# First loads on two queues, scores and values of half 1 in other banks, and head steps laid out unit by unit: a linear-attention and two-MLP kernel on one core

## The chip, the cores and the metric

The kernel runs on one core of a Trainium2 chip. The metric is device microseconds (us) of one execution, as a median of several; lower is better. The core has five engines that each run their own queue in order and wait for one another through semaphores: TensorE (PE; its weight loads are PEld), VectorE (DVE), ScalarE (ACT), GpSimd (POOL) and SyncE (SP), which issues most transfers. "Granted clock" is the share of TensorE's full speed that the chip allowed in a stretch; its two levels are 1.2 and 2.4 GHz, 0.5 and 1.0 in the rows.

## What is computed

Three stages follow one another. Inputs are q, k, v, alpha of 4 x 8 x 768 x 48 (batch, head, step, dimension); there are 3072 tokens of width 384.

```python
for t in range(S):                                   # gated linear attention
    state = alpha[:, :, t, :, None] * state + einsum(k[:, :, t], v[:, :, t])
    y[:, :, t] = einsum(q[:, :, t], state)
h = x @ w_in                                         # 384 -> 2048
P = a[0] + a[1]*h + a[2]*h**2 + a[3]*h**3
Q = 1.0 + abs(b[0])*abs(h) + abs(b[1])*h**2
x2 = (P / (Q + 1e-06)) @ w_out                       # 2048 -> 384
h = x2 @ w_in2                                       # 384 -> 1024
so = h * softmax(h); ln = normalise(so) * g_ln
out = ln @ w_out2                                    # 1024 -> 384
```

The weights arrive as 64-bit floats and are turned into a pair of 32-bit numbers, high and low, by integer steps on the chip; a product of two such pairs takes three matmuls.

## The kernel before

**Attention.** The 768 steps are cut into six chunks of 128 (c), and each chunk into two halves by batch, so half i has chunk i // 2; halves 2c and 2c + 1 must be done before chunk c goes on. A half's raw alpha, k and q come in by `a_load` (twelve transfers of 96 KB, all on SP), its v by `v_load`. Halves 0 and 1 are turned by TensorE (`a_turn`, products with a unit matrix), and DVE runs two scans per step over them. Halves 2 to 11 are turned by DVE itself (`a_prep`, which is `a_dve`: stream transposes, two long scans), then written to HBM and read back in another layout (`a_move_qk`, `a_move`). `a_pe` then makes the scores `sc`, copies them to `A` (ACT) and masks them (POOL), makes the values `y` and splits them into the chunk's activation `xt`, high part by ACT and low part by DVE, and updates the state `Sbd`. Eight PSUM banks are shared: three for `x2p`, three (`ps_hp`, tag "h") for the up-matmuls' `hp`, two (`ps_ap`, tag "at") for attention.

**First MLP.** 96 units follow, u = 16 c + f: unit u takes 128 of the 2048 columns for the 512 tokens of chunk c. `m_up` is nine matmuls into one bank, a rational function on ACT, DVE and POOL (three DVE steps in even units up to 22, lines 599, 604, 605; four in the others, lines 607, 610, 611, 612), and the pair `gh`, `gl`. `m_down` of the same unit is nine matmuls, laid four units later.

**Weights of the first MLP.** They come in four groups, one for each four units of a chunk (`w1_group`, seven tiles each: three of `w_in`, four of `w_out`). A tile is loaded as 64-bit numbers into a staging buffer, joined by three DVE instructions (`split_w`, lines 526, 529, 530), rounded by ACT and subtracted by POOL. There are two staging buffers `st`; while `stage["wide"]` is set, every second tile goes into a third one, `lent`, borrowed from a later group's place. In the kernel before, group 0, group 1 and the preparation of half 2 lie ahead of unit 0, and groups 2 and 3 lie in units 0 to 7.

**Order.** A planner sorts each engine's queue when the kernel is built, from the order of the code; `tc.issue_after` ties an instruction behind another. `half_steps(i)` lays one step of `a_pe(i)` and two of the next half's preparation into each unit from unit 2 of a half chunk on. After the units comes the second MLP, and out goes each tile of 128 tokens in four transfers (`n_out`).

## Time and profile before

| what | us |
|---|---|
| median of 3 runs | 805.89 (803.84 to 811.34) |
| profiled execution | 805.28 |
| its span | 803.5 |
| PE busy | 736.9 (92%) |
| DVE busy | 641.5 (80%) |
| ACT busy | 535.4 (67%) |
| POOL busy | 365.4 (45%) |

The profile is of one execution. Its own time is 1.8 us longer than its span, which is what lies around it. Busy shares are means over stages with different limits, so they have to be read stage by stage.

### The profile page before, as it was taken

Reading aid. Unit: us, or ns where it says so; the run is one execution under the profiler, and the core shown is the slowest. Engines: PE = TensorE matmul, PEld = TensorE weight load, DVE = VectorE, ACT = ScalarE, POOL = GpSimd, SP = SyncE. Lnnn points to the kernel's source line nnn. Section 1 sums busy time; section 2 is a strip of 40 time slices with the busy share of each in tenths; the row PEclk is TensorE's granted clock in tenths of the full one; section 3 lists DMA queues with packets and bytes.
Section 4 is the critical chain, followed back from the end, with each engine's and each line's share of the span. In section 5 each row is a group of like instructions: output and inputs, shape, how many; then the busy total and the mean of one; then the engine's idle time right before and its main releaser. Section 6 shows DMA issues by size and latency. Waiting matters only on the chain. (4 is left out here: it accounts for less than half of the span.)

```text
span 803.5 us, 13909 instructions
## 1 busy us (share of the span) xinstructions
PE 736.9 (92%) x4976; PEld 613.0 (76%) x4976; DVE 641.5 (80%) x1110; ACT 535.4 (67%) x983; POOL 365.4 (45%) x306
## 2 busy tenths in 40 slices
PE   4777786889999989999999999999999999999995
PEld 4665565667787767877777778888888989998995
DVE  6994999998889988979898976657877698777730
ACT  2324756678786868778887879788775555554631
POOL 3254757777654545445354334243233524352321
PEclk9757797999999998999999999999999999999998
DMA  7878229362764467363927151360013544541552
GB/s 171 174 176 241 86 84 231 100 163 76 225 162 147 89 199 174 116 151 110 226 80 179 45 124 29 117 278 0 1 40 100 143 105 110 134 113 48 130 128 61
DMA packets 87279, 101.75 MB, mean 127 GB/s; under 512 B 34464, under 2 KB 63136, under 8 KB 87200
## 3 DMA queue, kind: packets, MB, share of 16 engines
q1 hardware_dynamic: 87200, 100.77, 47.7%
q8 instruction: 41, 0.67, 0.4%
q14 instruction: 38, 0.31, 0.1%
HBM read 60.59 MB, written 27.56 MB: 110 GB/s over the span
## 5 line engine op out<-in xcount | busy, mean ns | idle before, releaser
L581 PE MATMUL hp<-xt,g 128*128 128x512 f32 x864 | 229.7, 408 | 24.9 <-DVE p L612 20.8
L581 PEld LDWEIGHTS hp<-xt,g 128*128 128x128 f32 x864 | 165.3, 195 | 68.0 <-DVE p L612 26.9
L615 POOL TENSOR_TENSOR gl<-p,gh 128x512 fp32r<-128x512 f32 x96 | 131.1, 1366 | 175.3 <-ACT gh L614 109.8
L627 PE MATMUL x2p<-gh,g 128*128 128x512 f32 x576 | 196.3, 397 | 0.0
L627 PEld LDWEIGHTS x2p<-gh,g 128*128 128x128 f32 x576 | 109.2, 190 | 25.4 <-issue 0.6
L627 PE MATMUL x2p<-gl,g 128*128 128x512 f32 x288 | 113.2, 393 | 0.4 <-POOL gl L615 0.4
L765 PE MATMUL op<-w2oh,room 128*128 128x384 f32 x384 | 101.6, 339 | 0.2 <-DVEq L1012 0.2
L757 POOL TENSOR_TENSOR room<-room,room 128x1024 fp32r<-128x1024 f32 x22 | 54.2, 2469 | 102.8 <-ACT room L756 87.8
L610 DVE SCALAR_TENSOR_TENSOR w<-w,co,hp 128x512 f32<-128x512 f32 x84 | 61.7, 735 | 42.7 <-ACT hp L609 42.4
L701 PE MATMUL h<-w2ih,x 128*128 128x512 f32 x288 | 90.8, 394 | 0.0
L588 ACT ACTIVATE p<-hp,co 128x512 f32<-128x512 f32 x96 | 66.0, 687 | 13.6 <-POOL gl L615 13.1
L607 DVE SCALAR_TENSOR_TENSOR p<-p,co,hp 128x512 f32<-128x512 f32 x84 | 61.6, 734 | 16.2 <-ACT p L588 15.8
L609 ACT ACTIVATE hp<-ah 128x512 f32<-128x512 f32 x84 | 50.2, 598 | 33.9 <-DVE p L607 33.3
L589 ACT ACTIVATE w<-ah,co 128x512 f32<-128x512 f32 x96 | 69.3, 722 | 4.4 <-DVE hp L611 4.2
L614 ACT ACTIVATE gh<-p 128x512 fp32r<-128x512 f32 x96 | 59.9, 624 | 18.3 <-DVE p L612 8.0
L765 PEld LDWEIGHTS op<-w2oh,room 128*128 128x128 f32 x384 | 70.1, 188 | 1.4 <-DVEq L1012 0.5
L586 ACT ACTIVATE ah<-hp 128x512 f32<-128x512 f32 x96 | 56.6, 590 | 13.7 <-PE hp L581 13.5
L765 PE MATMUL op<-w2ol,room 128*128 128x384 f32 x192 | 65.0, 338 | 0.0
L627 PEld LDWEIGHTS x2p<-gl,g 128*128 128x128 f32 x288 | 54.3, 189 | 12.6 <-POOL gl L615 0.8
L612 DVE SCALAR_TENSOR_TENSOR p<-p,co,hp 128x512 f32<-128x512 f32 x84 | 62.1, 740 | 1.0
L701 PEld LDWEIGHTS h<-w2ih,x 128*128 128x128 f32 x288 | 53.8, 188 | 11.8
L608 ACT ACTIVATE ah<-w,co 128x512 f32<-128x512 f32 x84 | 60.5, 720 | 1.3
(165 smaller groups left out, 1286.4 us busy)
## 6 DMA issues: line engine op xcount, KB each, us to landing
room<-room SPq DMA_DIRECT2D x96, 128.0 KB, 2.3
qk_d<-qk SPq DMA_DIRECT2D x10, 771.0 KB, 4.7
st<-in_moe_w_in_dram SPq DMA_DIRECT2D x15, 512.0 KB, 5.1
st<-in_moe_w_out_dram SPq DMA_DIRECT2D x20, 384.0 KB, 3.8
qks<-qk_d SPq DMA_DIRECT2D x20, 257.0 KB, 5.3
x<-x_d SPq DMA_DIRECT2D x18, 256.0 KB, 3.3
out_dram<-o SPq DMA_DIRECT2D x96, 48.0 KB, 1.6
ra<-in_alpha_dram SPq DMA_DIRECT2D x44, 96.0 KB, 3.3
```

What stands on the lines that cost most here:

```text
L581: last["PE", u] = nc.tensor.matmul(hp, lhsT=w[:, kt, 128 * o:128 * o + 128], rhs=xts[c][:, kt, xx, :], start=(kt == 0 and w is hi and xx = ...
L588: nc.scalar.activation(p, hp, AF.Square, bias=co[:, 7:8])
L589: nc.scalar.activation(w, ah, AF.Square, bias=co[:, 6:7])
L607: nc.vector.scalar_tensor_tensor(p, p, a1, hp, ALU.add, ALU.mult)
L608: nc.scalar.activation(ah, w, AF.Ln, bias=rest)
L610: nc.vector.scalar_tensor_tensor(w, w, rest, hp, ALU.add, ALU.mult)
L612: fin[u] = nc.vector.scalar_tensor_tensor(p, p, a0, hp, ALU.add, ALU.mult)
L614: last["ACT", u] = nc.scalar.activation(gh, p, AF.Copy)
L615: last["POOL", u] = nc.gpsimd.tensor_tensor(gl, p, gh[:].bitcast(F32), ALU.subtract)
L627: nc.tensor.matmul(x2ps[c][d], lhsT=w[:, o, 128 * d:128 * d + 128], rhs=gg, start=(f == 0 and w is hi and gg is gh), stop=(f == NF1 - 1 an ...
L701: nc.tensor.matmul(hp[:, 512 * n:512 * n + 512], lhsT=x2s[c][:, kt, x, CH * b:CH * b + CH], rhs=w2[w][:, kt, 512 * n:512 * n + 512], start ...
L765: nc.tensor.matmul(op, lhsT=x[:, 128 * f:128 * f + 128], rhs=w2[w][:, f, :], start=(f == 0 and x is hi and w == "oh"), stop=(f == NF2 - 1 ...
```

## The change

First, the raw loads of halves 0 and 1 go ahead of all weights, half of them on ACT's queue (`a_load` has a queue argument), and two of the four transfers of the very last output tile go out by ACT's queue. Second, nineteen instructions of `consts()`, which make coefficients from the six numbers of a and b, move from DVE to POOL, where one of them becomes two; one reciprocal stays on DVE. Third, half 1's scores and values take the three "h" banks. Fourth, weight groups 1, 2 and 3 lie in units 0 to 3, 4 to 7 and 8 to 11, each two tiles a unit, tied behind the last step of the unit before (`G1 = 1`); only groups 0 and 1 use the third staging buffer. Fifth, `script()` lays preparation (p), score and value steps (s) and moves (q, m, l) of halves 2 to 5 into named units up to 25; from unit 26 on the old rule goes on.

```diff
--- before.py
+++ after.py
@@ -70,17 +70,17 @@
     BETA = 2.0
     FASTS = (0, 20)
     GE = 80
-    NA = 5
     PRE = (1, 1, 0, 0)
     GP = 2
     GS = 2
-    G1 = 99
+    G1 = 1
     G2 = 3
     MIX = lambda u: u < 24 and u % 2 == 0
     EARLY = (9, 11, 13, 15)
     SKIP = (5, 7, 11)
     AHEAD = 3
     LATE = 2
+    FREE = 26
     U2, TP = 16, 0.3
     assert (B, H, D, CH) == (4, 8, 48, 128)
 
@@ -117,26 +117,28 @@
         nc.scalar.activation(cf[:, 0:1], bb[:, 1:2], AF.Abs)
         nc.scalar.activation(cf[:, 1:2], ab[:, 3:4], AF.Abs)
         nc.scalar.activation(lin[:, 0:1], bb[:, 0:1], AF.Abs)
-        nc.vector.tensor_scalar(sign, ab[:, 3:4], 0.0, 2.0, ALU.is_ge, ALU.mult)
...
-        nc.vector.tensor_scalar(cf, cf, C_MIN, None, ALU.max)
+        g = nc.gpsimd
+        g.tensor_scalar(sign, ab[:, 3:4], 0.0, 2.0, ALU.is_ge, ALU.mult)
...
+        g.tensor_scalar(cf, cf, C_MIN, None, ALU.max)
         nc.vector.reciprocal(rc, cf)
-        nc.vector.scalar_tensor_tensor(beta, lin, 0.5, rc, ALU.mult, ALU.mult)
-        nc.vector.tensor_tensor(t, beta, beta, ALU.mult)
...
+        g.tensor_tensor(beta, lin, rc, ALU.mult)
+        g.tensor_scalar(beta, beta, 0.5, None, ALU.mult)
+        g.tensor_tensor(t, beta, beta, ALU.mult)
...
@@ -249,7 +251,7 @@
             c, bp = divmod(i, 2)
             return c, 2 * bp + x // 2, 4 * (x % 2)
 
-        def a_load(i, names=("ra", "rk", "rq")):
+        def a_load(i, names=("ra", "rk", "rq"), queue=nc.sync):
             for x, (src, nm) in enumerate(((alpha, "ra"), (k, "rk"), (q, "rq"))):
                 if nm not in names:
                     continue
@@ -263,7 +265,7 @@
                     nc.gpsimd.memset(t[:, 16 * D:], 1.0)
                 for y in range(B):
                     c, b, h = slot(i, y)
-                    nc.sync.dma_start(
+                    queue.dma_start(
                         out=t[32 * y:32 * y + 32, :16 * D].rearrange("p (h x) -> p h x", h=4),
                         in_=src[b, h:h + 4, CH * c:CH * c + CH, :].rearrange("h (j r) d -> j h (r d)", r=4),
                     )
@@ -412,9 +414,10 @@
             c, bp = divmod(i, 2)
             vt = vts.pop(i)
             hf = half(i)
+            own = (ps_hp, "h") if i == 1 else (ps_ap, "at")
             A = {}
             for p in range(2):
-                sc = [ps_ap.tile([128, B, CH], F32, name="sc", tag="at") for j in range(2)]
+                sc = [own[0].tile([128, B, CH], F32, name="sc", tag=own[1]) for j in range(2)]
                 for x in range(B):
                     for j in range(2):
                         nc.tensor.matmul(
@@ -425,7 +428,7 @@
                 for j in range(2):
                     t = A[p, j] = ap_.tile([128, B, CH], F32, name="A", tag=f"A{p}{j}")
                     nc.scalar.activation(t, sc[j], AF.Copy)
-                    nc.gpsimd.affine_select(
+                    marks[i, "A"] = nc.gpsimd.affine_select(
                         out=t, in_=t, pattern=[[0, B], [1, CH]], compare_op=ALU.is_ge, fill=0.0, base=0,
                         channel_multiplier=-1,
                     )
@@ -434,7 +437,7 @@
             nc.gpsimd.tensor_copy(end, hf.ends[:, :, :, 0])
             ends = _view(end[:], 0, [[2, B], [1, 2], [0, D]])
 
-            y2 = [ps_ap.tile([128, n, 2 * CH], F32, name="y", tag="at") for n in (2, 1)]
+            y2 = [own[0].tile([128, n, 2 * CH], F32, name="y", tag=own[1]) for n in (2, 1)]
             begun = set()
 
             def put(m, x, w, r, last):
@@ -688,6 +691,7 @@
                 area[n] = moe_pool.tile([128, GW], F32R if n == 3 else F32, name=f"room{n}", tag=f"g{n}")
             return area[n][:, o:o + size]
 
+        NS = NCH * B
         lnT = {}
         st2 = {}
 
@@ -774,7 +778,7 @@
             nc.scalar.activation(o, op, AF.Copy)
             to = out.rearrange("(b c q j) d -> c q b j d", b=B, c=NCH, q=4)[c, qq]
             for b in range(B):
-                nc.sync.dma_start(out=to[b], in_=o[32 * b:32 * b + 32])
+                (nc.scalar if s == NS - 1 and b % 2 else nc.sync).dma_start(out=to[b], in_=o[32 * b:32 * b + 32])
 
         def n_tile(s):
             n_up(s)
@@ -794,28 +798,27 @@
 
         if fast:
             stage["wide"] = True
+            _run(a_load(0, ("ra",)), a_load(0, ("rk",), nc.scalar), a_load(1, ("ra",), nc.scalar))
+            _run(a_load(0, ("rq",)), a_load(1, ("rk",)), a_load(1, ("rq",), nc.scalar))
+            v_load(0)
+            nc.gpsimd.memset(Sbd, 0.0)
+            _run(a_turn(0))
+            pe0, pe1 = a_pe(0), a_pe(1)
+            take(pe0, 2)
+            _run(a_turn(1))
+            take(pe0, 1)
+            consts()
+            v_load(1)
+            take(pe1, 3)
             pre = w1_group(0)
-            _run(a_load(0))
-            take(pre, PRE[0])
-            v_load(0)
-            consts()
-            take(pre, PRE[1])
-            _run(a_load(1))
-            take(pre, PRE[2])
-            v_load(1)
-            take(pre, PRE[3])
-            nc.gpsimd.memset(Sbd, 0.0)
-            _run(a_turn(0), a_pe(0), a_turn(1), a_pe(1), pre)
-            clear()
-            pre = w1_group(1)
-            take(pre, NA)
+            with tc.issue_after(marks[1, 0, 0].ins):
+                take(pre, KT)
+                with tc.issue_after(marks[1, "A"].ins):
+                    _run(pre)
+            _run(pe0, pe1)
+            with tc.issue_after(marks[1, "A"].ins):
+                clear()
             _run(a_load(2, ("ra", "rk")))
-            with tc.issue_after(marks[0, 1].ins):
-                _run(a_prep(2))
-            _run(a_move_qk(2))
-            _run(a_enter(2), pre)
-            _run(a_load(3, ("ra", "rk")))
-            stage["wide"] = False
         else:
             for n in range(NG):
                 _run(w1_group(n))
@@ -854,15 +857,38 @@
                     return
                 yield
 
+        def script():
+
+            plan = {
+                2: "p2 p2", 3: "p2 p2", 4: "p2 p2 q2 m2 l3", 5: "p3 p3", 6: "p3 p3", 7: "p3 p3 s2", 8: "s2",
+                9: "s2 q3 l4", 10: "s2 m3", 12: "s3", 13: "s3", 14: "s3", 15: "s3", 16: "p4 p4", 17: "p4 p4",
+                18: "p4 p4 q4 m4 l5", 20: "p5 p5", 21: "s4 p5 p5", 22: "s4 p5 p5", 23: "s4 q5 l6", 24: "s4 m5",
+            }
+            ps = {i: a_prep(i) for i in (2, 3, 4, 5)}
+            ss = {i: a_pe(i) for i in (2, 3, 4)}
+            for u in range(FREE):
+                for w in plan.get(u, "").split():
+                    kind, i = w[0], int(w[1])
+                    with pin(GS if kind == "p" else GP):
+                        if kind in "ps":
+                            next((ps if kind == "p" else ss)[i], None)
+                        else:
+                            _run({
+                                "q": a_move_qk, "m": a_move, "l": lambda i: a_load(i, ("ra", "rk")),
+                            }[kind](i))
+                yield
+            for g in (*ps.values(), *ss.values()):
+                _run(g)
+
         split2 = w2_split() if fast else iter(())
         tp = 0.0
-        side = iter(())
+        side = script() if fast else iter(())
         tail = None
         prep = iter(())
         for u in range(NU + LAG):
             c, f = divmod(u, NF1)
             now[0] = u
-            if f % (NF1 // 2) == LATE and u < NU:
+            if f % (NF1 // 2) == LATE and FREE <= u < NU:
                 _run(side)
                 i = 2 * c + 2 + f // (NF1 // 2)
                 side = half_steps(i) if fast and i < NH else iter(())
@@ -877,7 +903,8 @@
                 if fast and u < NF1:
                     if f % 4 == 0:
                         _run(prep)
-                        prep = w1_group(f // 4 + 2) if f < 8 else iter(())
+                        stage["wide"] = f == 0
+                        prep = w1_group(f // 4 + 1) if f < 12 else iter(())
                     with later(G1):
                         take(prep, 1)
                 m_up(u)
@@ -907,7 +934,6 @@
         ph2["ps_o"] = end.enter_context(tc.tile_pool(name="ps_o", bufs=2, space=PSUM, side="left", reuse_waits="tile"))
         ph2["ha"] = end.enter_context(tc.tile_pool(name="ps_ha", bufs=1, space=PSUM, side="left", reuse_waits="tile"))
         ph2["hb"] = end.enter_context(tc.tile_pool(name="ps_hb", bufs=1, space=PSUM, side="left", reuse_waits="tile"))
-        NS = NCH * B
         done = 0
         cut = 0
         for s in range(len(EARLY), NS):
```

In the lists below, names are the program's with buffer numbers; line numbers of the changed kernel are 2 or 3 higher (526, 529, 530 become 529, 532, 533; 599 becomes 602; 128 becomes 129).

DVE in the second step of half 0. `co`, `ab`, `bad` are the coefficients, `ft` and `st` or `lent` a weight tile, `tp`, `Pp`, `Rp` the scans. Before:

```order
L530 SCALAR_TENSOR_TENSOR ft<-st,ft 128x512
L375 TENSOR_SCALAR qks<-Pp 128x4
L121 TENSOR_SCALAR co<-co 128x1
L126 TENSOR_SCALAR bad<-co 128x2
L383 TENSOR_TENSOR qks<-tp,Pp 128x4x128
L376 RECIPROCAL Rp<-qks 128x4
L122 TENSOR_TENSOR co<-ab,co 128x1
L123 TENSOR_TENSOR co<-ab,co 128x1
L124 TENSOR_TENSOR co<-ab,co 128x1
L127 TENSOR_SCALAR co<-co 128x2
L526 TENSOR_SCALAR ft<-lent_173 128x512
L378 SCALAR_TENSOR_TENSOR Rp<-tp,Rp,zero 128x127 x4
```

Now:

```order
L377 TENSOR_SCALAR qks<-Pp 128x4
L378 RECIPROCAL Rp<-qks 128x4
L380 SCALAR_TENSOR_TENSOR Rp<-tp,Rp,zero 128x127 x4
L129 RECIPROCAL co<-co 128x2
L384 TENSOR_TENSOR qks<-tp,Rp 128x4x128
L385 TENSOR_TENSOR qks<-tp,Pp 128x4x128
L376 SCALAR_TENSOR_TENSOR Pp<-tp,zero 128x128 x4
```

The coefficients and the first two weight tiles are gone from between half 0's steps; the reciprocal of `co` stands ahead of the two products that give half 0's k and q.

DVE where group 0 ends and group 1 begins, with the staging buffer `lent`. Before:

```order
L526 TENSOR_SCALAR ft_624<-lent2_173 128x512
L320 TENSOR_TENSOR qk_685<-qk_685,alT_111 128x2x3x128
L529 SCALAR_TENSOR_TENSOR ft_624<-lent2_173,ft_624 128x512
L290 STREAM_TRANSPOSE qk_685<-rq_678 128x2x4x32
L526 TENSOR_SCALAR ft_631<-st_632 128x512
L324 STREAM_TRANSPOSE alT_111<-qk_685 128x3x4x32 x2
L295 STREAM_TRANSPOSE qk_685<-rq_678 128x4x32 x2
L530 SCALAR_TENSOR_TENSOR ft_624<-lent2_173,ft_624 128x512
L529 SCALAR_TENSOR_TENSOR ft_631<-st_632,ft_631 128x512
L290 STREAM_TRANSPOSE qk_685<-rq_678 128x2x4x32
L530 SCALAR_TENSOR_TENSOR ft_631<-st_632,ft_631 128x512
L526 TENSOR_SCALAR ft_639<-lent2_173 128x512
```

Now (`u`, `Sbd` the state of half 0, `xt`, `y` the output of half 1):

```order
L532 SCALAR_TENSOR_TENSOR ft_535<-st_536,ft_535 128x384
L497 TENSOR_TENSOR Sbd_114<-u_570,end_361 48x8x48 x2
L533 SCALAR_TENSOR_TENSOR ft_535<-st_536,ft_535 128x384
L529 TENSOR_SCALAR ft_543<-lent2_273 128x384
L532 SCALAR_TENSOR_TENSOR ft_543<-lent2_273,ft_543 128x384
L533 SCALAR_TENSOR_TENSOR ft_543<-lent2_273,ft_543 128x384
L474 TENSOR_TENSOR xt_397<-y_466,xt_397 128x2x256
L529 TENSOR_SCALAR ft_550<-st_551 128x384
L474 TENSOR_TENSOR xt_397<-y_467,xt_397 128x256
L532 SCALAR_TENSOR_TENSOR ft_550<-st_551,ft_550 128x384
L533 SCALAR_TENSOR_TENSOR ft_550<-st_551,ft_550 128x384
L529 TENSOR_SCALAR ft_635<-lent2_273 128x512
```

Half 2's transposes and scans (`qk`, `alT`) are gone from between the tiles; two uses of `lent` are now two tiles apart with only half 1's output between them.

DVE in groups 2 and 3, where `hp`, `p`, `w` are a unit's function. Before, in units 5 to 8:

```order
L526 TENSOR_SCALAR ft_960<-st_961 128x512
L607 SCALAR_TENSOR_TENSOR p_1252<-p_1252,co_85,hp_1240 128x512
L612 SCALAR_TENSOR_TENSOR p_1111<-p_1111,co_85,hp_1099 128x512
L529 SCALAR_TENSOR_TENSOR ft_960<-st_961,ft_960 128x512
L605 SCALAR_TENSOR_TENSOR p_1192<-w_1191,hp_1180 128x512
L610 SCALAR_TENSOR_TENSOR w_1251<-w_1251,co_85,hp_1240 128x512
L530 SCALAR_TENSOR_TENSOR ft_960<-st_961,ft_960 128x512
L526 TENSOR_SCALAR ft_995<-st_996 128x512
L611 SCALAR_TENSOR_TENSOR hp_1240<-w_1251,hp_1240 128x512
L529 SCALAR_TENSOR_TENSOR ft_995<-st_996,ft_995 128x512
L612 SCALAR_TENSOR_TENSOR p_1252<-p_1252,co_85,hp_1240 128x512
L599 SCALAR_TENSOR_TENSOR hp_1275<-p_1287,co_85,hp_1275 128x512
```

Now, around unit 8's and 9's first steps:

```order
L532 SCALAR_TENSOR_TENSOR ft_1002<-st_1003,ft_1002 128x384
L533 SCALAR_TENSOR_TENSOR ft_1002<-st_1003,ft_1002 128x384
L602 SCALAR_TENSOR_TENSOR hp_1109<-p_1121,co_85,hp_1109 128x512
L610 SCALAR_TENSOR_TENSOR p_1189<-p_1189,co_85,hp_1177 128x512
L529 TENSOR_SCALAR ft_1030<-st_1031 128x384
L532 SCALAR_TENSOR_TENSOR ft_1030<-st_1031,ft_1030 128x384
L533 SCALAR_TENSOR_TENSOR ft_1030<-st_1031,ft_1030 128x384
L529 TENSOR_SCALAR ft_1101<-st_1102 128x512
L532 SCALAR_TENSOR_TENSOR ft_1101<-st_1102,ft_1101 128x512
L533 SCALAR_TENSOR_TENSOR ft_1101<-st_1102,ft_1101 128x512
L607 SCALAR_TENSOR_TENSOR hp_1109<-hp_1109,co_85,ah_1119 128x512
L613 SCALAR_TENSOR_TENSOR w_1188<-w_1188,co_85,hp_1177 128x512
```

Tiles that stood one by one between steps of units stand in rows of two and more, all through the two `st` buffers.

## Rows read from the trace of the kernel before

**Rows 1.** Busy time by stretch, all engines, granted clock and DMA share

```profile
core 0: us, PE busy (x) PEld busy (x) DVE busy (x) ACT busy (x) POOL busy (x), PEclk, DMA share, GB/s
0.00:6.50 6.50, 1.95 (x16) 1.60 (x16) 0.77 (x8) 2.31 (x3) 3.83 (x18) 1.00 0.56 145
6.50:37.20 30.70, 20.01 (x273) 17.10 (x272) 28.01 (x79) 7.46 (x20) 6.99 (x9) 0.85 0.89 189
37.20:61.60 24.40, 17.95 (x144) 15.47 (x144) 22.81 (x40) 7.84 (x18) 13.62 (x10) 0.56 0.68 166
61.60:86.80 25.20, 16.55 (x91) 13.13 (x91) 16.01 (x28) 11.09 (x21) 10.59 (x10) 0.71 0.73 200
86.80:187.60 100.80, 85.92 (x626) 67.33 (x626) 94.88 (x145) 69.70 (x128) 71.36 (x61) 0.92 0.51 131
187.60:261.70 74.10, 71.12 (x579) 57.40 (x578) 68.62 (x110) 58.64 (x108) 43.89 (x39) 0.98 0.55 160
```

**Rows 2.** Waits of DVE, 0 to 240 us: total, times, longest

```profile
DVE p L607 <- ACT p L588: 6.2, 5, 1.9
```

**Rows 3.** DVE in order of time, 58 to 92 us: start, duration, what

```profile
62.72 0.82 DVE L526 TENSOR_SCALAR ft<-lent 128x512 int32<-128x512 int32 x1 [2.28 <-DMA lent<-in_moe_w_in_dram]
63.57 0.69 DVE L529 SCALAR_TENSOR_TENSOR ft<-lent,ft 128x512 int32<-128x512 int32 x1
...
70.29 0.36 DVE L526 TENSOR_SCALAR ft<-lent 128x384 int32<-128x384 int32 x1 [1.89 <-DMA lent<-in_moe_w_out_dram]
...
78.73 1.13 DVE L526 TENSOR_SCALAR ft<-lent 128x384 int32<-128x384 int32 x1 [5.93 <-DMA lent<-in_moe_w_out_dram]
...
86.17 0.68 DVE L605 SCALAR_TENSOR_TENSOR p<-w,hp 128x512 f32<-128x512 f32 x1
```

**Rows 4.** DVE in order of time, 14 to 28 us, lines of consts()

```profile
16.15 0.17 DVE L126 TENSOR_SCALAR bad<-co 128x2 f32<-128x2 f32 x1 [1.22 <-ACT co L117]
...
16.91 1.18 DVE L122 TENSOR_TENSOR co<-ab,co 128x1 f32<-128x1 f32 x1
18.02 0.14 DVE L123 TENSOR_TENSOR co<-ab,co 128x1 f32<-128x1 f32 x1
18.09 0.59 DVE L124 TENSOR_TENSOR co<-ab,co 128x1 f32<-128x1 f32 x1
...
20.96 0.13 DVE L128 RECIPROCAL co<-co 128x2 f32<-128x2 f32 x1
...
25.73 0.73 DVE L134 TENSOR_TENSOR co<-co 128x2 f32<-128x2 f32 x1
...
27.15 0.48 DVE L136 TENSOR_TENSOR co<-co 128x2 f32<-128x2 f32 x1
```

**Rows 5.** PE in order of time, 40 to 120 us

```profile
48.17 4.86 PE L420 MATMUL sc<-lent 48*128 48x128 f32 x24 [2.06 <-DVE Sbd L494]
...
61.64 1.35 PE L581 MATMUL hp<-xt,g 128*128 128x512 f32 x3 [2.75 <-ACT xt L470]
...
92.32 1.34 PE L420 MATMUL sc<-qks 48*128 48x128 f32 x8
...
100.57 0.87 PE L444 MATMUL y<-qks,Sbd 128*32 128x128 f32 x24
...
103.77 2.36 PE L581 MATMUL hp<-xt,g 128*128 128x512 f32 x9
...
115.53 1.14 PE L481 MATMUL u<-vns,kns 128*64 128x48 f32 x32
```

**Rows 6.** DMA issues: queue, count, KB each, median us to landing

```profile
st<-in_moe_w_in_dram SPq DMA_DIRECT2D x15, 512.0 KB, 5.1
st<-in_moe_w_out_dram SPq DMA_DIRECT2D x20, 384.0 KB, 3.8
...
lent<-in_moe_w_out_dram SPq DMA_DIRECT2D x4, 384.0 KB, 5.7
```

**Rows 7.** SP's last transfers in order of time, 790 us to the end

```profile
791.10 6.82 SPq L777 DMA_DIRECT2D out_dram<-o  x8
```

More of the change, by code (lines that the diff above doesn't have):

```diff
@@ L135, in consts @@
[L135 to L139 removed]
+        g = nc.gpsimd
+        g.tensor_scalar(sign, ab[:, 3:4], 0.0, 2.0, ALU.is_ge, ALU.mult)
+        g.tensor_scalar(sign, sign, 1.0, None, ALU.subtract)
+        g.tensor_tensor(lin[:, 1:2], ab[:, 2:3], sign, ALU.mult)
@@ L141 @@
+        g.tensor_scalar(bad[:, 4 * NCH + 2:], t, BETA * BETA, None, ALU.is_gt)
+        g.tensor_scalar(beta, beta, B_MAX, -B_MAX, ALU.min, ALU.max)
+        g.tensor_tensor(t, beta, beta, ALU.mult)
+        g.tensor_tensor(base, base, rc, ALU.mult)
+        g.tensor_tensor(rest, base, t, ALU.subtract)
+        g.tensor_tensor(a0s, a0s, rc[:, 1:2], ALU.mult)
+        g.tensor_tensor(back, cf[:, 1:2], rc[:, 0:1], ALU.mult)
+        g.tensor_tensor(back, back, sign, ALU.mult)
     flag = const.tile([1, 1], I32, name="flag")
```

20 lines of the change are left out of this document (5 added, 15 removed).

## The prediction

> **What bounds the kernel now.** I read the stretches of busy time first and follow DVE and PE from row to row [rows 1]. From 187.6 us on both are full: PE 71.1 of 74.1 us, DVE 68.6. Ahead of that PE is not full: it is busy 85.9 of the 100.8 us from 86.8 to 187.6 and 54.5 of the 80.3 us from 6.5 to 86.8, and much of that at the lower clock (0.56 in 37.2 to 61.6, that is, mostly the 1.2 GHz level). DVE is the engine that is full: 28.0 of 30.7, 22.8 of 24.4, 94.9 of 100.8 us. It has one hole, the stretch from 61.6 to 86.8, where it works 16.0 of 25.2 us. So up to 187.6 us the time is DVE's work plus DVE's waits, and what the change saves ahead of that point is passed on to the end by engines that are full from there, in an order of work that the change leaves alone from unit 26 on.
>
> The waits of DVE come next. In the hole stand three waits of 2.28, 1.89 and 5.93 us, all for a transfer into `lent` [rows 3]; they make 10.1 of the 9.2 + 1.6 us that DVE idles from 37.2 to 86.8. After that only short waits of units for ACT are left (6.2 us in five, [rows 2]). Where the chain of PE looks bad it is not the bound: half 1's scores wait 2.06 us for a bank and run at 0.2 us each, and the first up-matmul starts at 61.64 after a wait for `xt` [rows 5], while DVE is busy 22.8 of 24.4 us in just that stretch. Starting unit 0 earlier is therefore worth nothing by itself; it lets DVE do units' steps and leave tiles and preparation for later, and the sum of its work stays.
>
> **The change part by part**, against the profiled execution's 805.3 us.
>
> *Removed: waits for `lent` in the hole, -10.1 us.* They came while half 2's results went to HBM and back and tiles were loaded with little else for DVE to do. Half 2's preparation now stands behind unit 2, so the round trip is not beside these loads. What replaces them is costed below.
>
> *Removed: coefficients on DVE, -4.0 us.* Four long ones take 1.18 + 0.59 + 0.73 + 0.48 = 3.0 us; fifteen short ones last 0.14 us but the next starts 0.07 us later (18.02 to 18.09), 1.05 us [rows 4]. The wait of 1.22 us for ACT ahead of line 126 goes too: -1.2. The other end: on POOL they are 20 instructions; if each holds up DVE by the 0.14 us that one lasts, 2.8 us come back and 1.2 us remain. The long ones show that DVE can be stretched while POOL works, but they ran beside POOL's large masks, and half 1's masks still run beside DVE's scans; I take -4.0. The Trainium skill (SBUF — State Buffer, "SBUF: two separate sides") says that GpSimd and a VectorE instruction with two SBUF inputs exclude each other from a shared port for a whole instruction. The 1.18 us of line 122 against 0.14 us of line 123 agree with it; by it the moved instructions would hold up DVE in their new place, and the sum below would be 2.8 us higher.
>
> *Removed: end of the program, -1.0 us.* The last eight output transfers leave SP in 6.8 us, 0.85 us each with waits [rows 7]. With two of the last four on another queue two fall out of the row, at most 1.7 us; no ACT-issued transfer is in this trace, so it can also be nothing. I take the middle.
>
> *Loads on two queues and their order: 0.* DMA is 0.56 busy in the first 6.5 us and 0.89 from there to 37.2 [rows 1], so there is little room that a second queue could fill, but half 1's raw data no longer stand behind weights. That brings half 1 forward; DVE's first work still waits for the first alpha, as before, and DVE has no other hole ahead of 37.2 us (28.0 of 30.7) that earlier data could fill.
>
> *Half 1's scores and values in the "h" banks: 0.* It takes the 2.06 us bank wait from PE [rows 5], which is not the bound there.
>
> *New: DVE waits for POOL at the reciprocal, +2.0 us.* It started at 20.96 [rows 4]. Ahead of it no longer stand the three joins and the next tile's first one (about 2.6 us) nor the coefficients and their wait (about 3.5 us by then): DVE is there at 14.8. The small loads of a and b now follow 24 raw loads instead of standing between them, so line 126's data are hardly earlier than the 16.15 of before; POOL has some five more short ones behind it: 16.9. Between 0 and 4.
>
> *New: two uses of `lent` close to one another, +2.5 us.* A `lent` load takes 5.7 us to land [rows 6]; between giving the buffer back and needing it DVE has about 3.0 us of work in the new list (two joins of 0.55 us, a first step of 0.36, two `xt` steps), so 2.7 us are missing, twice: once behind group 0's fourth tile, once ahead of group 1's first, where DVE waits for half 1's output anyway. 0 to 5.4.
>
> *New: groups 2 and 3 in rows, +3.0 us.* There are two `st` buffers; a tile takes 3.8 or 5.1 us to land [rows 6] from the moment that the one two before is given back, and where tiles stand next to one another DVE has 1.6 to 3.6 us of other work. I count five such places around units 8, 9, 11 and 12 with 0 to 2 us each, 0 to 9 in all. Before, tiles stood singly and no wait for an `st` load of note showed. I take a third: in three of the five places a unit's step or a transpose also stands between.
>
> *New: units 0 and 1 without cover, +2.0 us.* Their steps wait for ACT with fewer tiles to put between; the nearest row is the 1.2 us mean of the waits at line 607 [rows 2]. 0 to 6.2.
>
> Sum: -10.1 - 4.0 - 1.2 - 1.0 + 2.0 + 2.5 + 3.0 + 2.0 = -6.8, so 798.5 us for the profiled execution; the median stands 0.6 us above it: **799 us**.
>
> **The rivals.** *Hardly any new waits.* If the loads come in time in every place, only half of the new 9.5 us or less stays: -16.3 with none of it, 789; say 790 with 1 us. For it: DMA is only 0.51 busy from 86.8 on. Against: DVE has not been without a wait in any stretch.
>
> *The waits only move.* `lent` and `st` waits at their upper ends, 5.4 + 9 instead of 5.5: +8.9 on the forecast, 808; with one of the two at its end, 803 to 805. For it: all three large waits of before were of this kind, and the new lists put tiles closer together. Nothing measurable would remain.
>
> *PE becomes the bound behind unit 8 (slower).* Before, half 2's scores, values and state products lie between units 2 and 7 where PE had idle time: four times 1.34 us, 100.57 to 103.77, and 1.14 us [rows 5], 9.7 us. Now they lie behind unit 7, in front of halves 3 and 4, and between unit 7's and unit 8's last step DVE has 24 rows of tiles and half 3's preparation, in which PE runs out of work and of clock. PE idles 14.9 us from 86.8 to 187.6 [rows 1]. If less than 9.7 us of that can still be used behind unit 8, PE sets the time, the waits saved on DVE are lost, and the 9.7 us are added: 805.3 - 1.0 + 9.7 + 0.6 = 814.6. Against: DVE has to do the same work there anyway and is as full as PE. The point to look at is unit 0's last DVE step, which ended at 86.8 before [rows 3]: six tiles of about 2.1 us and half 2's preparation of about 11 no longer stand ahead of it, so for the forecast it must end by about 62, and unit 8's by about 133.
>
> *The change doesn't do what it says:* first up-matmul not earlier than 61.6, because the chain of half 1 is held by POOL or by loads. Then tiles of groups 1 to 3 are late as well; this goes with the slower case.
>
> **How the numbers follow.** A measurement of this kernel can tell about 1%, 8 us, from no change, so faster means under 797.8 and slower over 814. Forecast, 793 to 804: 0.40, nearly half of it under 797.8. No new waits, about 790: 0.25. Waits only move, 803 to 808: 0.19. PE the bound, about 814.6: 0.16, three quarters of it over 814. Faster 0.19 + 0.25 = 0.44; slower 0.12; between them 0.44. The range leaves a tenth out at each side: 787, a little under the second case since the coefficients' and end's terms can reach 1 us further, to 814, most of the slower case's way.
>
> **What the profile would show.** Right: first up-matmul near 44 us; unit 0's last DVE step near 62; DVE idle from 37 to 187 us some 5 us less than before; no coefficient on DVE but one, with a wait of about 2 us for POOL ahead of it; short DVE waits for `lent` and `st` loads around groups 0 to 3. Wrong: DVE waits for loads of over 8 us in all between units 7 and 12; or PE with no idle time from unit 8 on and later than before at unit 32 (261.7 us); or ACT held up by its own loads until half 1's scores wait for it, a wait that nothing in this trace can show.

## The result, and the profile after

The changed kernel takes **813.43 us** in the median of 20 runs (810.52 to 816.56) beside 805.92 us of the kernel before (20 runs, 802.61 to 812.88): a ratio of **1.0084, 95% interval 1.0061 to 1.0106**. It is 0.84% slower, 7.5 us. The forecast was 799 us. The profiled execution took 810.9 us, with a span of 809.1 us. Its line numbers are up to 4 higher than before: a tile's three joins are now L529, L532 and L533, the rounding on ACT is L539, the up-matmul L584.

The windows of the changed kernel over the stretches of [rows 1], with the same columns:

```profile
0.00:6.50 6.50, 0.00 (x0) 0.00 (x0) 0.76 (x7) 1.28 (x1) 2.43 (x16) 1.00 0.74 164
6.50:37.20 30.70, 25.93 (x366) 22.52 (x368) 25.71 (x63) 10.89 (x27) 11.21 (x30) 1.00 0.79 175
37.20:61.60 24.40, 16.66 (x151) 12.71 (x148) 19.27 (x32) 13.83 (x26) 13.99 (x15) 0.87 0.50 143
61.60:86.80 25.20, 20.70 (x75) 15.64 (x74) 24.73 (x39) 16.95 (x33) 14.96 (x13) 0.86 0.38 104
86.80:187.60 100.80, 73.79 (x564) 57.44 (x562) 89.87 (x133) 57.32 (x106) 62.64 (x55) 0.86 0.51 137
```

The hole of DVE from 61.6 to 86.8 us is closed (24.73 of 25.20, before 16.01). But DVE idles 5.0 us from 6.5 to 37.2 (before 2.7), 5.1 up to 61.6 (1.6) and 10.9 from 86.8 to 187.6 (5.9). From 37.2 to 187.6 that makes 16.5 us of idle time beside 16.7 before. And PE, which the change was to feed earlier, is busy 73.79 instead of 85.92 us in the last of these stretches, at a granted clock of 0.86 instead of 0.92.

The waits of DVE up to 240 us (the view of [rows 2]: total, times, longest):

```profile
DVE Pp L376 <- PE tp L365: 6.9, 1, 6.9
DVE hp L607 <- ACT ah L604: 4.7, 3, 2.6
DVE p L610 <- ACT p L591: 4.4, 2, 4.0
DVE qk L292 <- DMA rq<-in_q_dram: 2.2, 1, 2.2
DVE ft L529 <- DMA st<-in_moe_w_in_dram: 1.9, 1, 1.9
DVE ft L529 <- DMA st<-in_moe_w_out_dram: 1.9, 3, 1.3
...
DVE ft L529 <- DMA lent<-in_moe_w_in_dram: 0.9, 1, 0.9
...
DVE co L129 <- POOL co L128: 0.6, 1, 0.6
DVE ft L529 <- DMA lent<-in_moe_w_out_dram: 0.5, 1, 0.5
```

The 10.1 us of `lent` waits of [rows 3] are down to 1.4. In their place stand many: 6.9 us until the first alpha is transposed (4.91 before), 4.7 us for ACT at L607, where no such wait was before, 4.4 at L610 (before 6.2, [rows 2]), 3.8 us for `st`, 2.2 us for half 2's q.

Where a unit's steps stood can be followed by counting the last DVE instruction of each unit in order of time. Unit 0's last ends at 59.7 us (before 86.8), unit 7's at 102.4 (133.8), unit 8's at 134.9 (140.8), unit 16's at 187.5 (187.6), unit 32's at 274.7 (273.4). A lead of 27 to 31 us shrinks to 6 between two neighbouring units and to nothing by unit 16. ACT of the changed kernel in order of time shows how, behind unit 7's last step:

```profile
112.87 1.07 ACT L430 ACTIVATE A<-sc 128x512 f32<-128x512 f32 x2
120.00 0.52 ACT L539 ACTIVATE g<-ft 128x384 fp32r<-128x384 f32 x1 [6.07 <-DVE ft L533]
120.43 0.58 ACT L589 ACTIVATE ah<-hp 128x512 f32<-128x512 f32 x1
120.91 0.68 ACT L591 ACTIVATE p<-hp,co 128x512 f32<-128x512 f32 x1
...
123.55 0.61 ACT L430 ACTIVATE A<-sc 128x512 f32<-128x512 f32 x1
```

and PE beside it:

```profile
115.52 0.40 PE L630 MATMUL x2p<-gh,g 128*128 128x512 f32 x1
124.22 1.08 PE L447 MATMUL y<-qks,Sbd 128*32 128x128 f32 x16 [8.30 <-ACT A L430]
...
134.93 3.36 PE L584 MATMUL hp<-xt,g 128*128 128x512 f32 x7 [5.91 <-DVE p L608]
```

ACT's next instruction at 113.9 is the rounding of a tile whose joins stand behind half 3's preparation on DVE; it waits 6.07 us. The functions of unit 8, whose up-matmuls began at 100.7, and the second copies of half 2's scores are queued behind it. PE has half 2's values next in its own queue and waits 8.30 us for those copies; then unit 11's up-matmuls wait another 5.91 us for a PSUM bank, since unit 8's steps were late. DVE is full here: it works through all of ACT's 6.07 us and through 8.27 of PE's 8.30 us, on tiles and on half 3's preparation. Between unit 7's and unit 8's last steps (first line below) it is busy 29.11 of 32.50 us, and PE and ACT stand empty in line behind it. From there to unit 16's last step (second line; the third is the kernel before from unit 8's to unit 16's) it is the other way round:

```profile
102.40:134.90 32.50, 16.65 (x180) 13.05 (x178) 29.11 (x42) 14.15 (x29) 18.14 (x16) 0.88 0.71 188
134.90:187.50 52.60, 48.00 (x352) 37.55 (x352) 45.06 (x67) 34.87 (x65) 34.54 (x31) 0.88 0.37 92
140.80:187.60 46.80, 41.42 (x331) 32.81 (x331) 42.74 (x69) 34.69 (x65) 34.17 (x30) 1.00 0.48 122
```

PE is now nearly full, and at a lower granted clock; DVE idles 7.5 us where it idled 4.1. The longest of these waits, 4.00 us, can be followed through three engines:

```profile
162.24 1.08 PE L447 MATMUL y<-qks,Sbd 128*32 128x128 f32 x16 [4.15 <-ACT A L430]
164.51 3.65 PE L584 MATMUL hp<-xt,g 128*128 128x512 f32 x8
169.04 0.60 ACT L589 ACTIVATE ah<-hp 128x512 f32<-128x512 f32 x1 [3.59 <-PE hp L584]
170.25 0.75 DVE L610 SCALAR_TENSOR_TENSOR p<-p,co,hp 128x512 f32<-128x512 f32 x1 [4.00 <-ACT p L591]
```

PE waits for score copies. Behind that wait the granted clock is 0.55 from 164.5 to 168.2 us, and up-matmuls take 0.46 us each (0.24 in the nine from 102.95 us); ACT waits for them, and DVE for ACT. So the lead of 6 us at unit 8 is gone at unit 16: the engines are full in turns instead of together.

### The profile page after: what moved, and what is told of

It reads as the page before. It is cut to its first block, busy times and chain, and to the rows that moved or that the text cites. A ratio compares the mean times of both kernels' runs of the same rounds, so it can differ in the third digit from the quotient of the medians.

```text
span 809.1 us, 13900 instructions
## 1 busy us (share of the span) xinstructions
PE 734.6 (91%) x4976; PEld 607.6 (75%) x4976; DVE 640.8 (79%) x1091; ACT 536.4 (66%) x983; POOL 365.4 (45%) x326
## 5 line engine op out<-in xcount | busy, mean ns | idle before, releaser
L584 PE MATMUL hp<-xt,g 128*128 128x512 f32 x864 | 231.8, 410 | 25.8 <-DVE p L608 13.0
L584 PEld LDWEIGHTS hp<-xt,g 128*128 128x128 f32 x864 | 166.2, 196 | 69.2 <-DVE p L615 14.7
L630 PE MATMUL x2p<-gh,g 128*128 128x512 f32 x576 | 199.8, 402 | 7.1 <-ACT gh L617 6.5
L630 PEld LDWEIGHTS x2p<-gh,g 128*128 128x128 f32 x576 | 111.1, 193 | 34.2 <-ACT gh L617 6.9
L610 DVE SCALAR_TENSOR_TENSOR p<-p,co,hp 128x512 f32<-128x512 f32 x84 | 61.7, 735 | 14.9 <-ACT p L591 14.5
L617 ACT ACTIVATE gh<-p 128x512 fp32r<-128x512 f32 x96 | 60.0, 625 | 17.6 <-DVE p L615 10.1
```

What stands on the lines that cost most here:

```text
L584: last["PE", u] = nc.tensor.matmul(hp, lhsT=w[:, kt, 128 * o:128 * o + 128], rhs=xts[c][:, kt, xx, :], start=(kt == 0 and w is hi and xx = ...
L610: nc.vector.scalar_tensor_tensor(p, p, a1, hp, ALU.add, ALU.mult)
L617: last["ACT", u] = nc.scalar.activation(gh, p, AF.Copy)
L630: nc.tensor.matmul(x2ps[c][d], lhsT=w[:, o, 128 * d:128 * d + 128], rhs=gg, start=(f == 0 and w is hi and gg is gh), stop=(f == NF1 - 1 an ...
```

## The experiments

The kernel before was run beside each kernel. us are medians; "ratio" is to the kernel before, with its 95% interval.

**The head of the change alone.** Loads on two queues, order of halves 0 and 1, banks, coefficients on POOL, last output; half 2's preparation, the weight groups and the half steps as before.

```
+ half 2's preparation and group 1 in the head, as before
- side = script()
+ side = iter(())      # half_steps(i) from unit 2 on, as before
- G1 = 1, w1_group(f // 4 + 1)
+ G1 = 99, w1_group(f // 4 + 2)
```

> The changed head alone (loads on two queues, order of halves 0 and 1, half 1's banks, coefficients on POOL, last output on two queues), with half 2's preparation, weight groups 1 to 3 and the steps of half 3 and later where they stood before. Theory A (the head is a gain and the layout of units 0 to 25 loses it): faster than before, 798 to 804 us, unit 0's last DVE step near 75 and unit 8's ahead of 138. Rival B (the head itself costs, by the later first alpha and the new queue): 807 to 814 us, with unit 8's last step behind 140. Rival C (head and layout each do nothing, the loss arises behind unit 32): within 2 us of before at unit 32, and 808 to 813 at the end.

805.94 us, ratio 0.9997 (0.9979 to 1.0014), unit 0's last DVE step at 66.9, unit 8's at 136.9, first up-matmul of unit 32 at 260.0 (before 261.7). The head costs nothing by itself, but it brings nothing either. All three theories miss on the time.

**The layout of units 0 to 25 alone**, with the loads, banks and order of the old head:

```
+ the head of the code before (loads, halves 0 and 1, consts order)
  group 1 to 3 in units 0 to 11, G1 = 1, script()
```

> The changed layout of units 0 to 25 alone (groups 1 to 3 unit by unit, tied with G1 = 1, the plan of half steps), with the head, the loads, half 1's banks and the order of halves 0 and 1 as before (coefficients on DVE). Theory A: it is slower than the changed kernel by what the head saves, 815 to 822 us, with a gap of over 25 us between unit 7's and unit 8's last DVE steps. Rival B: 800 to 806 us. Rival C: within 3 us of the changed kernel, 810 to 816.

815.87 us, ratio 1.0106 (1.0079 to 1.0133); 28.4 us between unit 7's and unit 8's last steps. Against what the expectation says, the coefficients stayed on POOL in this kernel (401 DVE instructions up to unit 32's last step, as in the changed kernel; 420 before), and so did the last output on two queues. The time lies in theory A's range and at the edge of C's. With the head alone at 0.9997 it says that the layout is where the change loses.

**Weights as before; and only the tie undone.**

```
- prep = w1_group(f // 4 + 1) if f < 12 else iter(())
+ prep = w1_group(f // 4 + 2) if f < 8 else iter(())
- G1 = 1
+ G1 = 99                                    # the second kernel: only this
+ group 1 in the head, as before
```

> The changed kernel with the three weight groups where they were in the code before: group 1 in the head, groups 2 and 3 in units 0 to 7, not tied to units (G1 = 99); head and plan of half steps stay. Theory A1 (the late, tied weight groups cost): 800 to 806 us, the gap between unit 7's and unit 8's last DVE steps falls from 32 to under 15 us. Rival A2 (the plan of half steps costs, not the weights): 811 to 815 us, the gap stays over 25 us or moves to the next group.

> The changed kernel with one number back, G1 = 99, so that no tile is tied to the unit before; the groups stay in units 0 to 11. Theory A1 with the tie as the cause: as the kernel with the weights where they were, 800 to 807 us. If the place in the code and not the tie counts: 810 to 815. If neither counts (A2): 811 to 815 with DVE idle from 87 to 188 us as in the changed kernel, 10 to 13 us.

808.10 us, ratio 1.0022 (1.0000 to 1.0044), gap of units 7 and 8 14.2 us; and 813.75 us, 1.0080 (1.0055 to 1.0105), gap 11.5 us. The gap can go without the time going: it only moves to group 3, between units 11 and 12 (25.2 us in the second). It looked as if the weights' place cost 5.7 us. That did not stand, see the corners below.

**Coefficients alone**, on the kernel before:

```
- nc.vector.tensor_scalar(sign, ab[:, 3:4], 0.0, 2.0, ALU.is_ge, ALU.mult)
+ nc.gpsimd.tensor_scalar(sign, ab[:, 3:4], 0.0, 2.0, ALU.is_ge, ALU.mult)
...
```

> The kernel before with one edit: the coefficients on POOL (19 of 20 off DVE, as in the change). Theory of the sum (DVE's work up to 187.6 us sets the time): 4 us less, 800 to 803 us, unit 16's last DVE step near 183.5. Rival (the time saved on DVE is given back to waits and to DVE instructions that are stretched while POOL works): 804.5 to 808 us, DVE idle up to 187.6 us longer by 3 to 5 us.

804.35 us beside 807.37, ratio 0.9961 (0.9932 to 0.9991), by that 3.1 us less; unit 16's last step at 181.3. The sum had -4.0, -1.2 and +2.0 for them and their waits, together -3.2: about right here, within an interval of 0.7 to 5.5 us.

**A join left out** of each of the 28 tiles of groups 0 to 3, in the kernel before and in the changed one, to see what DVE's work is worth (the weights then lack their sign and top exponent bit):

```
-                 nc.vector.scalar_tensor_tensor(fi, w32[:, :, 1], -0x40000000, fi, ...)
+                 if keep is not None:
+                     nc.vector.scalar_tensor_tensor(fi, w32[:, :, 1], -0x40000000, fi, ...)
```

> The kernel before, with the second of the three joins of each of the 28 weight tiles of groups 0 to 3 left out (the floats then lack their sign and top exponent bit). It takes some 22 us of work from DVE ahead of 187.6 us and nothing from the other engines. Theory D (DVE's work sets the time up to there): 783 to 790 us. Rival P (the order in which engines wait for one another sets it, and DVE's busy share shows queueing rather than a bound): 797 to 806 us, the work turned into DVE idle time.

> The changed kernel with the same second join left out in the 28 tiles. Theory D: 22 us less than the changed kernel, 790 to 797 us, and the distance to the same edit of the kernel before stays at +6 to +9 us. Theory A (tiles in front of units' steps are what loses time in the new layout): shorter tiles take away most of that distance, 783 to 791 us, within 2 us of the kernel before with the same edit.

793.33 us, ratio 0.9813 (0.9744 to 0.9882), and 799.43 us, 0.9906 (0.9874 to 0.9938). Up to unit 32's last step the joins take 52.4 instead of 76.9 us of DVE, 24.5 less, and the end moves by 0.0187 x 807.4 = 15.1: **six tenths of a microsecond for each of DVE's**, with a wide interval (9.5 to 20.7 us). That is between the two theories. The distance of the two kernels stays (0.93% with two joins, 0.84% with three), so nothing here says that it hangs on how long the tiles in front of the units' steps are.

**Second profiled executions** of both kernels, unchanged.

> The changed kernel unchanged, for a second profiled execution. If the wait for a tile of the second half's weights and the low clock at 391 to 398 us belong to the new order: up-matmul of unit 56 again 6 to 9 us behind that of the kernel before (393.8). If they are an accident of one execution: 2 to 5 us behind, while unit 32 is again within 1 us of 262.9.

> The kernel before unchanged, for a second profiled execution. If the part behind unit 32 was short by accident in the first one (543.6 us from unit 32's first up-matmul to the end, against 544.2 to 548.9 in the other eight): 545 to 548 us now, and the distance of the changed kernel lies ahead of unit 32 for the most part. If it is the order: 543 to 544.5 again.

814.13 and 804.76 us. Unit 32's first up-matmul starts at 266.0 and 260.0 (first executions 262.9 and 261.7), unit 56's at 400.8 in the changed kernel: 7.0 us behind 393.8, so the loss is there again, though by another way. From unit 32 to the end the changed kernel needs 548.0 and 548.1 us, the kernel before 543.6 and 544.8. Neither expectation fits well: of the distance 1 to 6 us lie ahead of unit 32 by the execution, 3 to 4.5 behind it.

**One queue for the first loads**, in the changed head alone:

```
- _run(a_load(0, ("ra",)), a_load(0, ("rk",), nc.scalar), a_load(1, ("ra",), nc.scalar))
+ _run(a_load(0, ("ra",)), a_load(0, ("rk",), nc.sync), a_load(1, ("ra",), nc.sync))
...
```

> The changed head alone (as in the first run), but all first loads on SP's queue, in the same order. Theory Q (the second queue makes the first alpha land later, 3.4 instead of 2.2 us after its issue, and everything behind it): first transposes on PE at 4.5 to 5.0 instead of 6.56 us, and 2 to 3 us less than the changed head alone, 802.5 to 805 us beside a kernel before of 806 to 807. Rival (the first 37 us have slack, as the prediction's term of 0 for the queues says): first transposes earlier, time within 1 us of the changed head alone.

799.05 us, ratio **0.9918** (0.9890 to 0.9945): 0.8% less than with two queues, more than the theory said. PE's first transposes in order of time, in the head alone with two queues:

```profile
6.75 1.98 PE L365 MATMUL tp<-ident,ra 128*64 128x128 f32 x16 [6.75 <-DMA lent<-in_q_dram]
```

and with one:

```profile
4.79 1.98 PE L365 MATMUL tp<-ident,ra 128*64 128x128 f32 x16 [4.79 <-DMA ra<-in_alpha_dram]
```

A start 2 us earlier grows to 6 by unit 32 (260.0 and 253.8). The order of the engines' instructions from unit 2 on also comes out another way when the first loads stand elsewhere, so the 6 us are not the queue's alone.

**Half 1 alone on the second queue**, on the kernel before with the coefficients on POOL; **and half 1's loads on it only behind ACT's first work on half 0**, in the changed head:

```
- _run(a_load(1))
+ _run(a_load(1, queue=nc.scalar))
```

```
- _run(a_load(0, ("ra",)), a_load(0, ("rk",), nc.scalar), a_load(1, ("ra",), nc.scalar))
...
+ _run(a_load(0))
...
+ with tc.issue_after(marks[0, "w"].ins):     # ACT's first work on half 0's alpha
+     _run(a_load(1, queue=nc.scalar))
```

> The kernel before with the coefficients on POOL and half 1's first loads on ACT's queue, half 0's first and alone on SP's. Theory Q: the first alpha lands later here too, by 0.5 to 1.2 us, and what half 1 gains is worth nothing by itself: 804 to 807 us, no better than the coefficients alone (0.996 of the kernel before). Rival (half 1's wait of 5.1 us at 19.8 us cost time): 799 to 802.5 us.

> The changed head alone, half 0's loads on SP's queue alone and half 1's on ACT's queue behind ACT's first work on half 0's alpha, so that they start when that has landed. If the late first alpha is what the second queue costs: first transposes at 4.5 to 5.0 us, 797 to 801 us, as with one queue or better. If ACT's time for issuing, or the traffic, costs: 803 to 807 us.

809.12 us, ratio 1.0026 (0.9999 to 1.0053), 0.65% worse than without the queue; the first transposes start at 6.86 us although half 0's loads are alone on SP. And 802.36 us, 0.9966 (0.9940 to 0.9991), with the first transposes at 4.60: with alpha on time the head lies between its two forms. The late alpha is a part of the queue's cost, not the whole; ACT, in whose queue half 1's loads stand until 15.7 us here, is the other candidate, and that was not separated.

**The plan only up to unit 17**, weights as before.

```
-                16: "p4 p4", 17: "p4 p4", 18: "p4 p4 q4 m4 l5", 20: "p5 p5", ... 24: "s4 m5",
+                14: "s3 p4 p4", 15: "s3 p4 p4", 16: "p4 p4 q4 l5", 17: "m4",
-    FREE = 26
+    FREE = 18
```

> The changed kernel with the weights where they were before, and the plan only for halves 2 and 3 and the preparation of half 4; from unit 18 on the steps of half 4 and later as before. Theory (the rest of the loss, 2 us against the changed head alone, lies in the plan's units 18 to 25): 804 to 806 us, from unit 16's last DVE step to unit 32's first up-matmul 74 to 75 us instead of 75.7. Rival (it lies in units 2 to 17): 807 to 809 us.

807.29 us, ratio 1.0014 (0.9984 to 1.0045); 75.6 us from unit 16's last step to unit 32's first up-matmul. The later units of the plan are not the seat of the loss.

**The corners.** Three things can each be as before or as changed: the queues, the place of the weight groups, and the plan of half steps. The four kernels still missing:

> The changed kernel with all first loads on SP's queue, in the same order; all else of the change stays. If the queue's cost and the layout's cost add: the ratio to the kernel before falls from 1.008 by the 0.008 that the queue cost the changed head, to 0.999 to 1.002 (805 to 808 us). If the lead at the start is lost in the layout whatever it is: 811 to 814 us.

> The changed kernel with the weights where they were before and one queue for the first loads. If both costs add: 0.8% less than the same with two queues (1.002), 799 to 803 us, and no faster than the changed head with one queue (0.992), so that the plan of half steps brings nothing. If the plan brings something once the queue is out of the way: 793 to 798 us.

> The changed kernel without the plan of half steps: half 2's preparation in the head and the steps of half 3 and later by the rule of the code before, but the weight groups 1 to 3 unit by unit and tied (G1 = 1) as changed; first loads on two queues. If the plan is what costs (and not where the weights stand): as the changed head alone, 804 to 808 us (0.9997). If the weights' place costs (5.7 us between two earlier runs): 809 to 814 us.

> The same with the first loads on SP's queue alone. If the plan is what costs: as the changed head with one queue, 798 to 802 us (0.992). If the weights' place costs: 803 to 808 us.

They measured 808.92 us (1.0036, 1.0008 to 1.0065), 812.47 (1.0080, 1.0051 to 1.0109), 802.87 (0.9976, 0.9951 to 1.0000) and 800.05 (0.9932, 0.9909 to 0.9956). The two without the plan came out where "the plan is what costs" put them, the first a little lower. Of the two with it, 808.92 lies just above the range for costs that add, and 812.47 is 9 us above both of its ranges. All eight, as ratios to the kernel before, in each the rest of the head as changed:

| | weights as before, two queues | weights as before, one queue | weights as changed, two queues | weights as changed, one queue |
|---|---|---|---|---|
| half steps as before | 0.9997 | 0.9918 | 0.9976 | 0.9932 |
| the plan | 1.0022 | 1.0080 | 1.0084 (the change) | 1.0036 |

**The plan** costs in each column: 0.25, 1.62, 1.08 and 1.04%, 1.0% or **8.0 us** in the mean. The first of the four is within the noise of its pair, the other three are clear of it. Which part of the plan costs was not separated, but for its units from 18 on, which the kernel with the plan only up to unit 17 clears: 1.0014 beside 1.0022. **The second queue** costs 0.79, 0.44 and 0.48% in three pairs and gains 0.58% in the fourth (weights as before, with the plan). **The weights' place** goes both ways (-0.21, +0.14, +0.62, -0.44%), 0.03% in the mean: the theory that it costs falls.

**Coefficients back on DVE in the head with one queue.**

```
- g.tensor_scalar(sign, ab[:, 3:4], 0.0, 2.0, ALU.is_ge, ALU.mult)
+ nc.vector.tensor_scalar(sign, ab[:, 3:4], 0.0, 2.0, ALU.is_ge, ALU.mult)
...
```

> The changed head alone with one queue and the coefficients back on DVE; the order on DVE from unit 3 on is the same. By the sum (4.0 us, bound 1.2): 2.5 to 5 us more than with them on POOL, 802 to 804.5 us. Rival (in this head DVE has slack there): within 1 us, 798 to 800 us.

799.98 us, ratio 0.9921 (0.9894 to 0.9949): no difference from 0.9918. The same DVE work, some 5 us by unit 32's last step here (240.6 after 235.4), is worth 3 us in one head and nothing in another.

The three fastest kernels: the changed head with one queue and the old order behind it (0.9918), the same with the weights as changed (0.9932), and the same with the coefficients on DVE (0.9921).

**Where the plan's 8 us show.** DVE has the same work behind it at unit 32's last step (the same 401 instructions in every kernel of the table, of which a window may cut off the last). The window from 0 to that step of the changed kernel (columns as in [rows 1]):

```profile
0.00:274.70 274.70, 221.17 (x1787) 175.17 (x1788) 238.06 (x400) 167.42 (x310) 157.75 (x170) 0.92 0.59 155
```

and of the kernel with the same weights, one queue and no plan:

```profile
0.00:265.30 265.30, 220.65 (x1787) 175.81 (x1788) 234.91 (x401) 166.91 (x310) 159.34 (x169) 0.92 0.61 160
```

| | step ends | DVE busy | DVE idle |
|---|---|---|---|
| mean of the four with half steps as before | 267.7 | 236.4 | 31.3 |
| mean of the four with the plan | 274.0 | 238.3 | 35.7 |

Of 6.3 us that the plan has cost by then, 4.3 are more waiting of DVE, for the same work; the waiting is longer in each of the four pairs (2.9 to 5.9 us). The other 2.0 are busy time, which goes both ways (-5.5 to +7.1) and is not settled. The waiting lies where the chain above lies: from unit 8's to unit 16's last step DVE idles 3.3, 2.1, 4.0 and 5.1 us in the four kernels without the plan and 6.4 to 7.5 in the four with it. PE's waits differ in kind. PE's waits from 62 to 262 us (total, times, longest), in the changed kernel:

```profile
PE y L447 <- ACT A L430: 12.4, 2, 8.3
PE hp L584 <- DVE p L608: 7.3, 3, 5.9
PE x2p L630 <- ACT gh L617: 6.5, 1, 6.5
```

and without the plan (weights as changed, one queue):

```profile
PE hp L584 <- DVE alT L304: 22.2, 2, 12.0
PE hp L584 <- DVE p L615: 8.7, 7, 3.4
...
PE x2p L630 <- ACT gh L617: 0.5, 1, 0.5
```

Without the plan PE waits as long, but for DVE itself. With it a part of the wait goes through ACT's copies of scores, which stand behind DVE's work in their turn: 12.4 us (11.5 in the second execution), 9.3 with one queue, 10.3 with the weights as before and one queue, 8.6 with the old head, 3.8, 4.4 and 1.0 in the others and 1.2 with the join left out. Of the eleven executions without the plan ten have no such wait and one, with the join left out, has 0.6 us. The kernel with 1.0 us of it (the tie undone, 1.0080) is as slow as the change and the one with 3.8 is not, so the wait is a mark of the plan that is clear in seven of nine executions and not a measure of its cost. That the chain shown above makes the whole of the 8 us is not shown either: with the weights as before it is partly `st` loads that DVE waits for there.

## Why the prediction was wrong

The step that failed is the one with which the sum begins: the `lent` waits' 10.1 us were counted as gone because "Half 2's preparation now stands behind unit 2", and what that move and the plan around it put in front of PE and ACT stood in the sum at nothing (one rival had it, at 9.7 us). By the corners the plan costs 8.0 us in the mean. With half 2's preparation left in the head and the half steps under the old rule, the rest of the change makes 0.9976, which is 804.0 us on the median before, and with one queue besides 0.9932, 800.4 us, near the forecast 799. The `lent` waits go there too (2.2 us up to 187.6 us in the kernel without the plan and with one queue): they did not need the plan. What the trace of the change shows in place of the gain are engines that are full in turns: DVE works through its part of the moved work while PE stands empty, and then waits itself, 7.5 us instead of 4.1 from unit 8's to unit 16's last step, while PE works at a lower granted clock. The prediction called anything within 1% no change; the interval here is a quarter of that to each side, so 0.84% is a loss. Point by point:

- **`lent` waits, -10.1, and what replaces them (+2.5, +3.0): the size was right.** Up to unit 32's last step DVE's waits at tiles for loads and POOL fall from 12.1 to 6.4 us, 5.7, where the sum had 4.6. But waits for ACT's unit functions rise from 10.7 to 13.8, for half data from HBM from 0 to 2.5, for PE's transposes and products from 6.0 to 10.1. All of DVE's waits together are 34.3 us after 30.5.
- **Coefficients, -4.0 and -1.2, with +2.0 at the reciprocal:** -3.1 alone on the kernel before, 0 in the head with one queue. The wait at the reciprocal is 0.63 us where 2.0 stood.
- **The end, -1.0: nothing against it.** From PE's last matmul to the end it takes 8.9 us in the mean of fifteen executions with the split (8.15 to 9.90) and 10.2 in five without (8.76 to 11.66); the two ranges overlap.
- **Loads on two queues, 0: wrong**, +2 us at the first transposes and 3.5 to 6.4 us at the end in three of four pairs (in the fourth the second queue gains). The step that said "DVE's first work still waits for the first alpha, as before" did not ask when that alpha lands. DMA is only 0.56 busy in the first 6.5 us [rows 1], but that room is not free: with a second set under way the share is 0.74 and the first alpha lands later.
- **Half 1's banks, 0:** not tried.
- **Units 0 and 1 without cover, +2.0:** 2.65 us ahead of unit 0's L607, as sized.
- **"The sum of its work stays", and what is saved ahead of 187.6 is passed on whole:** the joins left out pass on some six tenths. At that rate, an estimate, even the sum of -6.8 was worth some -4.
- **The signs** given for a right forecast were met where they speak of the head: first up-matmul 42.4 (near 44), unit 0's last step 59.7 (62), unit 8's 134.9 (133). They were no evidence, since units had been pulled ahead of tiles and preparation that were still owed. The one that counts work, DVE idle from 37 to 187 us some 5 us less, failed: 16.5 after 16.7. Of the signs against it, PE nearly without idle time behind unit 8 (4.6 of 52.6 us up to unit 16's last step) and later at unit 32 (262.9 after 261.7) came close.
- **The rival "PE becomes the bound behind unit 8"** gave 814.6, and the time came out at 813.4. Much of its mechanism is there: PE runs out of work between unit 7's and unit 8's last steps (16.65 of 32.50 us), and behind them, up to unit 16's, it idles 4.6 us, less than the 9.7 that the rival asked for, at a granted clock of 0.88 instead of 1.00. But PE is not the only bound: over the whole stretch from 86.8 to 187.6 us it idles 27.0 us, more than before (14.9), and behind unit 8 it still waits 4.15 us for ACT's copies. No run shows the 9.7 us by themselves, and that the time came so near is in part luck.

Open: 3 to 4.5 us of the distance arise behind unit 32, where the order on DVE is the same from about unit 38. In the first execution a wait of DVE of 2.13 us for a tile at 388.1 is followed by PE waits of 1.75 and 1.17 us and a granted clock of 0.64 from 391.2 to 398.0; in the second the clock there is 1.00, and it is behind by as much. By the corners little of it is the plan's: from unit 32's first up-matmul to the end the four kernels with it take 546.9 us in the mean and the four without it 545.6, while that matmul starts at 262.6 and 256.3. What the rest is, is not settled. Nor is why the second queue gains with the plan and the old weights; every edit of the first 100 us also reorders units 3 to 25, and single pairs of such kernels scattered by some half a per cent.

## What to carry to other kernels

A lead in a milestone is a gain only where the same work lies behind it: compare kernels at a point with the same count of instructions done, and split the difference there into busy and idle time. When several engines execute in order, moved work is paid for by what stands behind it in each queue, also where an engine is full in one stretch and waits in the next, and a wait that disappears on the busiest engine says little until the next one in line has been named. And where an edit reshuffles the order of everything after it, one pair of runs doesn't attribute a half per cent; take each part away in all combinations.

## What the runs showed of the hardware

Two sets of loads at once slow each other: an alpha transfer of 96 KB needs 2.2 us in the median to land with one queue (2.1 to 2.3 in eleven executions) and 3.4 to 3.6 with two (nine), and the first transposes move from 4.5 to 4.9 us to 6.5 to 6.9. ACT, which issues the second set, starts its first instruction on data at 10.64 us instead of 4.52, although its data have landed by 6.42 us. The Trainium skill (DMA: Bandwidth & Descriptors, "Issuing engines are not separate DMA queues") says that transfers started by different engines share the same DMA engines and interleave, and that a second engine saves only time for issuing. These runs agree, and add that the saving can be paid back by the first transfer that everything waits for.

DVE's joins take longer beside POOL: the third one (both shapes, all 42 tiles) takes 0.58 us in the mean of 22 in the kernel before that have no POOL instruction beside them (0.51 to 0.69), and 1.37 us in the mean of 7 that have one beside them all the time (0.76 to 1.76); in the changed kernel it is 0.60 us (22) and 1.22 us (8, 0.56 to 1.97). The Trainium skill (SBUF — State Buffer, "SBUF: two separate sides") has a lock on a shared port that would do this; what the rows show is a factor of about two in the mean, not in each instruction, and that a duration from a row holds for that row's neighbours.
